# Attention and feed-forward on one core: a third buffer for scores and pieces, a second for the feed-forward step, values laid out so that nothing is shifted, and a new plan

## The chip, the core and the metric

The kernel runs on one core of one Trainium2 chip. Its engines work side by side, each through its own instructions in order: PE (TensorE, matmuls; PEld are its weight loads), DVE (VectorE), ACT (ScalarE), POOL (GpSimd), and SP (SyncE), which here issues every DMA. The metric is device time in microseconds of one execution. Sizes below are partitions x elements.

## The reference

```python
def _attn_ref(q, k, v, tau):                      # q, k, v: (8, 8, 576, 64)
    scale = 1.0 / np.sqrt(q.shape[-1])
    scores = scale * np.matmul(q, k.transpose(0, 1, 3, 2))
    thresh = np.max(scores, axis=-1, keepdims=True) - tau
    scores = np.where(scores >= thresh, scores, -1000000000.0)
    scores = scores - np.max(scores, axis=-1, keepdims=True)
    attn = np.exp(scores)
    attn = attn / (np.sum(attn, axis=-1, keepdims=True) + 1e-09)
    return np.matmul(attn, v)

def _moe_ref(x, w_in, w_out, s, b):               # x: (4608, 512), w_in: (512, 2048)
    h = x @ w_in
    r = np.maximum(h, 0.0)
    g = s * (r * r) + b
    return g @ w_out                              # w_out: (2048, 512)
```

x is the attention's output with the heads side by side. w_in and w_out come in as 64-bit floats, which the kernel takes apart itself.

## The kernel before

**Attention.** There are 8 batches of 4 pairs of heads. Batch 0 goes in plain fp32 (`plain_tile`, 36 tiles); batches 1 to 7 (`split_tile`, 9 tiles of 128 queries a pair, 252 in all) with numbers split in two: k and q as an fp32r part and the rest of it, the weights of the attention and v as two fp16 pieces. A split tile runs: scores on PE into bank `s` or `t` (L485); row maximum on DVE (L488); threshold on POOL (L490); exp on ACT into `em` (L492); threshold and sum on DVE (L494), which frees the bank; 1/sum by POOL and DVE (L497, L499); the first fp16 piece on ACT into `en` (L500), the second on DVE (L502); then a transposing DMA on SP (L507) brings both pieces, 1152 columns, into nine blocks of `ea` or `eb`. `em` and `en` have two buffers each, taken by tiles in turn.

**Values.** With 576 keys the first piece ends in the middle of the fifth block, so the second piece's keys sit 64 partitions off. `Values.prepare` therefore lays v out in five blocks and copies them, by three DMAs a head (L394), into four more blocks shifted by 64 partitions. `with_v` (L518) multiplies nine blocks of pieces by nine of v into bank `pv`, which ACT and DVE take out (L523, L525).

**Loads.** `Head.load` (L311) brings k and q of one head twice each, to partitions 0 to 63 and 64 to 127. `Head.prepare` splits them with ACT and POOL (L332 to L345).

**Feed-forward.** x goes in 18 blocks of 256 rows, 16 steps each, so 288 steps. A step (`Block.step`): 12 matmuls into bank `h` (L698), ReLU on ACT into the one buffer `g` (L702), square (L705), rounded part `gh` (L706), the rest `gl` on POOL (L707; DVE in the last block), then 6 matmuls into bank `o` (L713). `finish` (L727, L731) writes 256 rows out. `bias_t`, `oo` and `g` are buffers of their own.

**The order.** `Plan` holds every operation with its engine, a cost in ns (time on the engine, time to the result), what it reads and writes, and when it is due. `run` places them five times in a list schedule, forwards and backwards, keeps the shortest plan and emits all operations in its order. `HANDOVER` is the time from one engine's result to another engine's start. The plan knows buffers by the names in its lists; the order of accesses to one tile or bank is enforced apart from it by semaphores that the build puts in.

Of the kernel before, what the change touches and what calls it, by code (L numbers as in the profile page):

```python
# [9 lines left out]
F32 = mybir.dt.float32  # L10
F32R = mybir.dt.float32r
# [24 lines left out]
class Plan:  # L36
# [7 lines left out]
    HANDOVER = 50  # L44
# [95 lines left out]
def tile_attention_ffn(ctx: ExitStack, tc: tile.TileContext, qT, kT, v, tau, w_in, w_out, s, b, out):  # L140
# [3 lines left out]
    P = 128  # L144
# [28 lines left out]
    bias_t = const("bias_t", [P, DM])  # L173
# [3 lines left out]
    en, em = ([const(f"{n}{i}", [P, S + 1]) for i in range(2)] for n in ("en", "em"))  # L177
# [42 lines left out]
    def split_buffers():  # L220
# [10 lines left out]
        claim(["e32", "oo0", "oo1"] + [("x", 2, c, j, u) for c in range(NC) for j in range(2) for u in range(2)], lambda: None)  # L231
# [17 lines left out]
    def dma(kb, fn, r, w, at):  # L249
        plan.add("SP", (max(550, kb * 3.6), 2200 + kb * 3.6), fn, r, w, at)  # L250


    def transfer(rows, fn, r, w, at):
        plan.add("SP", (1250, 3400), fn, r, w, at)
# [42 lines left out]
    class Head:  # L297
        def __init__(self, i, bi, h, q0, q1, tail):
            self.i, self.bi, self.h, self.j, self.q0, self.q1, self.tail = i, bi, h, h % 2, q0, q1, tail
            self.v, self.kvs = vt[i % 3], [("v", i % 3, n) for n in range(4)]  # L300

        def load(self, at):

            q0, q1 = self.q0, self.q1
            self.parts = [], []

            def put(which, name, buf, cols, ap, kb):
                for o in 0, D:
                    keys = [(name, o, c) for c in range(cols.start // T, cols.stop // T)]
                    self.parts[which].extend(keys)  # L310
                    dma(kb, lambda o=o: nc.sync.dma_start(out=buf[o:o + D, cols], in_=ap), [], keys, at)  # L311

            put(0, "rk", rk, slice(0, S), kT[self.bi, self.h], 144)
            q1_ = S if self.tail and q1 == M else q1
            put(1, "rq", rq, slice(q0, q1_), qT[self.bi, self.h, :, q0:q1_], (q1_ - q0) // 4)
            if self.tail and q1_ < S:
                put(1, "rq", rq, slice(M, S), qT[self.bi, self.h, :, M:S], 16)

        def prepare(self, at):
            pk, pq = self.parts  # L320
            j = self.j
            q0, m = self.q0, self.q1
            n = m - q0
# [8 lines left out]
            act((580, 675), lambda: nc.scalar.copy(out=khi(), in_=rk), pk, [f"khi{j}"], at)  # L332
            pool((1420, 1450), lambda: nc.gpsimd.tensor_tensor(out=klo(), in0=rk, in1=khi().bitcast(F32), op=ALU.subtract),  # L333
                 pk + [f"khi{j}"], [f"klo{j}"], at)

            parts = [(slice(q0, m), qs[j][:, 0:n], f"q{j}", (60 + n, 160 + n), (100 + 2.3 * n, 130 + 2.3 * n))]
            if self.tail:
                parts.append((slice(M, S), qt[:, j, j * T:(j + 1) * T], f"qt{j}", (150, 245), (250, 280)))
            cut = [slice(q0, S)] if m == M and self.tail else [x[0] for x in parts]
            pool((130 + 1.25 * sum(x.stop - x.start for x in cut), 160 + 1.25 * sum(x.stop - x.start for x in cut)),  # L340
                 lambda: [nc.gpsimd.tensor_scalar(out=rq[:, x], in0=rq[:, x], scalar1=scale, scalar2=1.0, op0=ALU.mult,
                                                  op1=ALU.mult) for x in cut], pq + ["bound"], pq, at)
            for cs, dst, key, ca, cd in parts:
                act(ca, lambda dst=dst, cs=cs: nc.scalar.copy(out=dst, in_=rq[:, cs]), pq, [key], at)
                pool(cd, lambda dst=dst, cs=cs: nc.gpsimd.tensor_tensor(  # L345
                    out=dst[D:P], in0=rq[D:P, cs], in1=dst[D:P].bitcast(F32), op=ALU.subtract), pq + [key], [key], at)

    class Values:
# [5 lines left out]
        def load(self, at):  # L354
            bi, h2 = self.hds[0].bi, slice(self.hds[0].h, self.hds[0].h + 2)
            dma(256, lambda: nc.sync.dma_start(out=rv[:, :, 0:NQ, :].rearrange("p h t d -> p h (t d)"),
                                               in_=v[bi, h2, 0:M, :].rearrange("h (p t) d -> p h (t d)", t=NQ)),
                [], ["rv"], at)
            dma(32, lambda: nc.sync.dma_start(out=rv[0:T, :, NQ, :], in_=v[bi, h2, M:S, :].rearrange("h p d -> p h d")),
                [], [("rv", 1)], at)  # L360
# [626 lines left out]
```

## Time and profile before

| | us |
|---|---|
| median of 3 runs | 1317.81 (1310.39 to 1318.17) |
| the profiled run | 1319.79 |
| its span | 1318.0 |
| PE busy | 1234.2 (94%) |
| ACT busy | 998.6 (76%) |
| DVE busy | 910.3 (69%) |
| POOL busy | 761.0 (58%) |

The mean granted clock is 0.967. A group's row names line, engine, operation, out<-in, shapes and count, then busy time and mean ns of one, then the engine's idle time before these instructions and what ended most of it. A busy PE need not be at its peak: matmuls are pipelined. Which idle time matters is read by stage.

### The profile page before, as it was taken

What the parts mean: (1) busy time and instruction counts of PE and PEld (TensorE: products, weight loads), DVE (VectorE), ACT (ScalarE), POOL (GpSimd) and SP (SyncE); (2) the same over time, 40 slices, a digit from 0 to 9 for tenths busy, and PEclk for the clock granted to TensorE, in tenths of its full rate; (3) what the DMA queues carried; (4) which work ended last, traced back from release to release, by engine and by line L of the source; (5) the groups of instructions that cost most, each with busy time, mean ns of one, the idle gap of its engine ahead of it and who ended that gap; (6) DMA issues with size and microseconds to landing.
All of it is one profiled execution on the core that took longest, in us unless ns stands there. A gap on an engine that the chain in (4) does not pass through costs nothing.

```text
span 1318.0 us, 25354 instructions
## 1 busy us (share of the span) xinstructions
PE 1234.2 (94%) x8205; PEld 978.4 (74%) x8205; DVE 910.3 (69%) x2041; ACT 998.6 (76%) x2059; POOL 761.0 (58%) x1272
## 2 busy tenths in 40 slices
PE   9999988887999899999999999999999999999998
PEld 6667666766777677777878778878787777777776
DVE  6766888878777777777677778777777777750111
ACT  5676787877888887788788888878887987874543
POOL 2245376666776666667577666667666776632310
PEclk9778789998999999999999999999999999999999
DMA  9452036776667667766556667666766666640000
GB/s 295 146 160 65 10 76 136 147 134 147 134 137 133 127 139 137 144 126 137 99 130 129 141 126 136 130 140 128 136 119 139 112 141 125 123 80 1 17 17 17
DMA packets 362997, 155.30 MB, mean 118 GB/s; under 512 B 316784, under 2 KB 341360, under 8 KB 362864
## 3 DMA queue, kind: packets, MB, share of 16 engines
q1 hardware_dynamic: 362864, 153.69, 55.7%
q8 instruction: 64, 1.05, 0.3%
q14 instruction: 69, 0.57, 0.1%
HBM read 61.61 MB, written 9.44 MB: 54 GB/s over the span
## 4 chain that ended last, share of the span: by engine, by line
PE 51%; ACT 10%; DMA 9%; issue 8%; DVE 8%; POOL 8%; SPq 2%; POOLq 0%; DVEq 0%; ACTq 0%
PE o L713 18%; PE h L698 17%; PE pv L518 5%; DMA eb<-en 3%; PE t L485 3%; PE s L485 3%; POOL gl L707 2%; DMA ea<-en 2%; ACT en L500 2%; PE pv L463 2%; DMA rq<-in_q_dram 2%; DVE em L494 2%; PE s L420 2%; DVE en L502 2%; DVE st L488 2%
## 5 line engine op out<-in xcount | busy, mean ns | idle before, releaser
L698 PE MATMUL h<-xp,iw 128*128 128x256 f16 x3456 | 434.4, 276 | 10.5 <-ACT g L702 9.1
L698 PEld LDWEIGHTS <-iw 128*128 128x128 f16 x3456 | 323.3, 99 | 103.9 <-issue 60.4
L713 PE MATMUL o<-ow,gh 128*128 128x512 f32 x1152 | 384.0, 414 | 3.2 <-ACT gh L706 1.8
L707 POOL TENSOR_TENSOR gl<-g,gh 128x256 fp32r<-128x256 f32 x272 | 212.0, 779 | 188.7 <-ACT gh L706 149.4
L502 DVE SCALAR_TENSOR_TENSOR en<-em,st,en 128x576 f16<-128x576 f32 x252 | 235.1, 935 | 59.2 <-ACT en L500 56.9
L500 ACT ACTIVATE en<-em,st 128x576 f16<-128x576 f32 x252 | 194.0, 771 | 64.6 <-DMA eb<-en 27.5
L713 PE MATMUL o<-ow,gl 128*128 128x512 f32 x576 | 231.3, 402 | 7.4 <-POOL gl L707 6.9
L702 ACT ACTIVATE g<-h,wback 128x256 f32<-128x256 f32 x288 | 135.2, 469 | 117.8 <-PE h L698 89.9
L713 PEld LDWEIGHTS o<-ow,gh 128*128 128x128 f32 x1152 | 193.8, 191 | 28.5 <-ACT gh L706 2.7
L713 PEld LDWEIGHTS o<-ow,gl 128*128 128x128 f32 x576 | 108.9, 189 | 41.2 <-POOL gl L707 16.9
L490 POOL TENSOR_SCALAR st<-st,bound 128x1 f32<-128x1 f32 x252 | 104.7, 417 | 50.9 <-DVE st L488 36.2
L518 PEld LDWEIGHTS <-v 128*128 128x128 f16 x1008 | 93.1, 99 | 54.3 <-issue 15.7
L494 DVE SCALAR_TENSOR_TENSOR em<-t,st,em 128x576 f32<-128x576 f32 x126 | 102.5, 814 | 34.9 <-ACT em L492 16.0
L497 POOL TENSOR_SCALAR st<-st 128x1 f32<-128x1 f32 x252 | 79.9, 317 | 80.6 <-DVE em L494 50.8
L705 ACT ACTIVATE g<-g 128x256 f32<-128x256 f32 x288 | 119.7, 416 | 6.5
L706 ACT CAST gh<-g 128x256 fp32r<-128x256 f32 x288 | 116.0, 403 | 6.7 <-PE o L713 0.6
L494 DVE SCALAR_TENSOR_TENSOR em<-s,st,em 128x576 f32<-128x576 f32 x126 | 102.5, 814 | 22.4 <-ACT em L492 13.9
L492 ACT ACTIVATE em<-t,st 128x576 f32<-128x576 f32 x126 | 92.8, 737 | 22.5 <-DVE en L502 15.6
L488 DVE TENSOR_REDUCE st<-s 128x1 f32<-128x576 f32 x126 | 94.4, 749 | 20.6 <-PE s L485 19.7
L492 ACT ACTIVATE em<-s,st 128x576 f32<-128x576 f32 x126 | 92.8, 736 | 19.7 <-DVE en L502 12.0
L488 DVE TENSOR_REDUCE st<-t 128x1 f32<-128x576 f32 x126 | 94.4, 749 | 17.5 <-PE t L485 15.8
L333 POOL TENSOR_TENSOR k<-rk,k 128x576 fp32r<-128x576 f32 x56 | 80.9, 1445 | 25.3 <-ACT k L332 24.0
(158 smaller groups left out, 1853.1 us busy)
## 6 DMA issues: line engine op xcount, KB each, us to landing
rq<-in_q_dram SPq DMA_DIRECT2D x112, 144.0 KB, 2.9
rk<-in_k_dram SPq DMA_DIRECT2D x112, 144.0 KB, 2.9
iw<-in_moe_w_in_dram SPq DMA_DIRECT2D x16, 512.0 KB, 6.9
ow<-in_moe_w_out_dram SPq DMA_DIRECT2D x16, 512.0 KB, 7.2
out_dram<-oo SPq DMA_DIRECT2D x32, 256.0 KB, 2.8
rv<-in_v_dram SPq DMA_DIRECT2D x28, 256.0 KB, 3.2
v<-v SPq DMA_DIRECT2D x112, 64.0 KB, 2.1
ea<-en SPq DMA_TRANSPOSE x140, 3.2
```

The lines of the kernel that those rows point to most:

```text
L488: dve((745, 825), lambda: nc.vector.tensor_reduce(out=top, in_=ps, axis=mybir.AxisListType.XY, op=ALU.max, negate=True), [bk], [(ks_, 0)], ...
L492: act((740, 835), lambda: nc.scalar.activation(out=halves, in_=ps, func=AF.Exp, bias=top, scale=1.0), [bk, (ks_, 0)], [em_k], i - 0.5)
L494: dve((890, 970), lambda: nc.vector.scalar_tensor_tensor(out=halves, in0=ps, scalar=line, in1=halves, op0=ALU.is_ge, op1=ALU.mult, accum_o ...
L500: act((690, 785), lambda: nc.scalar.activation(out=pieces[:, 0:S], in_=ex, func=AF.Copy, scale=unit), [em_k, (ks_, 3)], [en_k], i)
L502: dve2((790, 880), lambda: nc.vector.scalar_tensor_tensor(out=pieces[:, S:2 * S], in0=ex, scalar=unit, in1=pieces[:, 0:S], op0=ALU.mult, o ...
L518: nc.tensor.matmul(ps, hd.v[:, n], e[:, n], start=(n == 0), stop=(n == 8))
L698: nc.tensor.matmul(ps, wi[w][f][:, c * P:(c + 1) * P], x[:, h, c, :], start=(c == 0 and i == 0), stop=(c == NC - 1 and i == 2))
L702: act((290, 385), lambda: nc.scalar.activation(out=g, in_=ps, func=AF.Relu, scale=wback[:, f:f + 1]), ["h", ("wback", f)], ["g"], at)
L705: act((290, 390), lambda: nc.scalar.activation(out=g, in_=g, func=AF.Square), ["g"], ["g"], at)
L706: act((310, 405), lambda: nc.scalar.copy(out=hi, in_=g), ["g"], [f"gh{k}"], at)
L707: do((715, 750), lambda: eng.tensor_tensor(out=lo, in0=g, in1=hi.bitcast(F32), op=ALU.subtract), ["g", f"gh{k}"], [f"gl{k}"], at)
L713: nc.tensor.matmul(bank["o"][:, t, :], a[:, ts_], w, start=(f == 0 and i == 0), stop=(f == NF - 1 and i == 2))
```

## The change

- `em` and `en` have three buffers in `split_tile`; `plain_tile` keeps two.
- The second piece is written in two DVE instructions, the last 64 keys first and then the other 512. Its keys then lie on the same partitions as the first piece's, apart from the fifth block, whose lower half belongs to the second piece. v's last 64 keys are loaded to both halves of the fifth block (`rv`), the products take block `n % 5`, and the shifting DMAs are gone.
- k and q of two heads come with one DMA per half of the partitions.
- `g` has two buffers, in the unused halves of the tiles of the converted w_in (`spare`), and `h` is taken in two halves of its bank in turn. Bias and output buffers lie in such halves too; the second buffer of the plain tiles' transposed scores lies in `rv`.
- `HANDOVER` is 150, and most costs in the plan are other numbers (one of them is shown).

```diff
-    HANDOVER = 50
+    HANDOVER = 150
...
-    en, em = ([const(f"{n}{i}", [P, S + 1]) for i in range(2)] for n in ("en", "em"))
+    en, em = ([const(f"{n}{i}", [P, S + 1]) for i in range(3)] for n in ("en", "em"))
...
-    vt = [const(f"v{i}", [P, 9, P], F16) for i in range(3)]
+    vt = [const(f"v{i}", [P, 5, P], F16) for i in range(3)]
...
-    rk, rq, rv = const("rk", [P, S]), const("rq", [P, S]), const("rv", [P, 2, 5, D])
+    rk, rq, rv = const("rk", [P, 2, S]), const("rq", [P, 2, S]), const("rv", [P, 2, 5, D])
...
-    oo = const("oo", [P, 2, DM])
-    gb = const("g", [P, NB])
...
+    def spare(f):
+
+        return lazy["wi", f][:, 2:4].bitcast(F32).rearrange("p a b -> p (a b)")
...
-            def put(which, name, buf, cols, ap, kb):
-                for o in 0, D:
-                    keys = [(name, o, c) for c in range(cols.start // T, cols.stop // T)]
-                    self.parts[which].extend(keys)
-                    dma(kb, lambda o=o: nc.sync.dma_start(out=buf[o:o + D, cols], in_=ap), [], keys, at)
...
+            if not self.j:
+                h2 = slice(self.h, self.h + 2)
+                for n, buf, ap in ("rk", rk, kT), ("rq", rq, qT):
+                    for o in 0, D:
+                        load(288, lambda buf=buf, ap=ap, o=o: nc.sync.dma_start(
+                            out=buf[o:o + D], in_=ap[self.bi, h2].rearrange("h d s -> d h s")),
+                            [], [(n, o, j) for j in range(2)], at)
...
+            for u in range(2):
+                load(32, lambda u=u: nc.sync.dma_start(out=rv[u * T:(u + 1) * T, :, NQ, :],
+                                                       in_=v[bi, h2, M:S, :].rearrange("h p d -> p h d")),
+                     [], [("rv", 1 + u)], at)
...
-                for n, (r, c, r_, c_) in enumerate((
-                        (slice(0, T), slice(5, 9), slice(T, P), slice(0, 4)),
-                        (slice(T, P), slice(8, 9), slice(0, T), slice(4, 5)),
-                        (slice(T, P), slice(4, 8), slice(0, T), slice(0, 4)))):
-                    dma(64, lambda t=t, r=r, c=c, r_=r_, c_=c_: nc.sync.dma_start(out=t[r, c, :], in_=t[r_, c_, :]),
-                        keys[0:1], [keys[1 + n]], at)
...
-        ex, em_k = em[i % 2][:, 0:S], f"em{i % 2}"
-        pieces, en_k = en[i % 2].bitcast(F16)[:, 0:2 * S], f"en{i % 2}"
+        ex, em_k = em[i % 3][:, 0:S], f"em{i % 3}"
+        pieces, en_k = en[i % 3].bitcast(F16)[:, 0:2 * S], f"en{i % 3}"
...
-        act((740, 835), lambda: nc.scalar.activation(out=halves, in_=ps, func=AF.Exp, bias=top, scale=1.0),
+        act((636, 740), lambda: nc.scalar.activation(out=halves, in_=ps, func=AF.Exp, bias=top, scale=1.0),
...
-        dve2((790, 880), lambda: nc.vector.scalar_tensor_tensor(
-            out=pieces[:, S:2 * S], in0=ex, scalar=unit, in1=pieces[:, 0:S], op0=ALU.mult, op1=ALU.subtract),
-            [em_k, en_k, (ks_, 3)], [en_k], i)
+        def rest():
+            for o, c in (slice(S, S + T), slice(M, S)), (slice(S + T, 2 * S), slice(0, M)):
+                nc.vector.scalar_tensor_tensor(out=pieces[:, o], in0=ex[:, c], scalar=unit, in1=pieces[:, c],
+                                               op0=ALU.mult, op1=ALU.subtract)
+        dve2((800, 885), rest, [em_k, en_k, (ks_, 3)], [en_k], i)
...
-                nc.tensor.matmul(ps, hd.v[:, n], e[:, n], start=(n == 0), stop=(n == 8))
+                nc.tensor.matmul(ps, hd.v[:, n % 5], e[:, n], start=(n == 0), stop=(n == 8))
...
-            ps, g, hi, lo = bank["h"][:, 0:NB], gb, gh[k], gl[k]
+            ps, hi, lo, h, kg = bank["h"][:, k * NB:(k + 1) * NB], gh[k], gl[k], f"h{k}", f"g{k}"
+
+            def g():
+                return spare(k)[:, 0:NB]
```

More of the change, by code (lines that the diff above doesn't have):

```diff
@@ L249, in dma, with load @@
     def dma(kb, fn, r, w, at):
-        plan.add("SP", (max(550, kb * 3.6), 2200 + kb * 3.6), fn, r, w, at)
+        plan.add("SP", (max(600, kb * 3.6), 2200 + kb * 3.6), fn, r, w, at)
+    def load(kb, fn, r, w, at):
+        plan.add("SP", (620, 2300 + kb * 4.5), fn, r, w, at)
     def transfer(rows, fn, r, w, at):
-        plan.add("SP", (1250, 3400), fn, r, w, at)
+        plan.add("SP", (1350, 3600), fn, r, w, at)
     class Plain:
@@ L355, in load @@
             bi, h2 = self.hds[0].bi, slice(self.hds[0].h, self.hds[0].h + 2)
[L356 to L360, printed above, removed]
+            load(256, lambda: nc.sync.dma_start(out=rv[:, :, 0:NQ, :].rearrange("p h t d -> p h (t d)"),
+                                                in_=v[bi, h2, 0:M, :].rearrange("h (p t) d -> p h (t d)", t=NQ)),
+                 [], ["rv"], at)
@@ L569, in w @@
         def w(u):
-            t = sb("io"[u] + f"w{f}", [P, 2, DM], (F16, F32R)[u])
+            t = sb("io"[u] + f"w{f}", [P, 4 - 2 * u, DM], (F16, F32R)[u])
+            if not u:
+                lazy["wi", f] = t
             for h in range(2):
@@ L634, in products @@
                 nc.tensor.matmul(bank["h"], ones, wo[h][f], start=(n == 0), stop=(n == 7))
-        pe(8, DM, products, [(f"w{f}", "o") for f in fs] + ["ones"], ["h"], at)
+        hs = ["h0", "h1"]
+        pe(8, DM, products, [(f"w{f}", "o") for f in fs] + ["ones"], hs, at)
         if k == 0:
-            act((520, 620), lambda: nc.scalar.copy(out=bias_t, in_=bank["h"]), ["h"], ["bias"], at)
+            act((465, 565), lambda: nc.scalar.copy(out=spare(2), in_=bank["h"]), hs + [("w2", "i")], ["bias"], at)
         else:
-            dve((620, 700), lambda: nc.vector.tensor_tensor(out=bias_t, in0=bank["h"], in1=bias_t, op=ALU.add),
-                ["h", "bias"], ["bias"], at)
+            dve((660, 745), lambda: nc.vector.tensor_tensor(out=spare(2), in0=bank["h"], in1=spare(2), op=ALU.add),
+                hs + ["bias"], ["bias"], at)
         if k == 3:
-            act((560, 660), lambda: nc.scalar.mul(out=bias_t, in_=bias_t, mul=b_t), ["bias", "b"], ["bias"], at)
+            act((510, 610), lambda: nc.scalar.mul(out=spare(2), in_=spare(2), mul=b_t), ["bias", "b"], ["bias"], at)
     count = dict(stage=0, step=0)
@@ L696, in products @@
                 for c in range(NC):
-                    for i, (w, h) in enumerate(((0, 0), (0, 1), (1, 0))):
-                        nc.tensor.matmul(ps, wi[w][f][:, c * P:(c + 1) * P], x[:, h, c, :], start=(c == 0 and i == 0),
+                    for i, (w, u) in enumerate(((0, 0), (0, 1), (1, 0))):
+                        nc.tensor.matmul(ps, wi[w][f][:, c * P:(c + 1) * P], x[:, u, c, :], start=(c == 0 and i == 0),
                                          stop=(c == NC - 1 and i == 2))
-            plan.add("PE", (12 * 0.427 * NB, 12 * 0.427 * NB + 170), products, self.kx + [(f"w{f}", "i")], ["h"], at)
-            act((290, 385), lambda: nc.scalar.activation(out=g, in_=ps, func=AF.Relu, scale=wback[:, f:f + 1]),
-                ["h", ("wback", f)], ["g"], at)
+            plan.add("PE", (12 * 0.427 * NB, 12 * 0.427 * NB + 170), products, self.kx + [(f"w{f}", "i")], [h], at)
+            act((357, 473), lambda: nc.scalar.activation(out=g(), in_=ps, func=AF.Relu, scale=wback[:, f:f + 1]),
+                [h, ("wback", f), (f"w{k}", "i")], [kg], at)
             eng, do = (nc.vector, dve2) if self.last else (nc.gpsimd, pool)
-            act((290, 390), lambda: nc.scalar.activation(out=g, in_=g, func=AF.Square), ["g"], ["g"], at)
-            act((310, 405), lambda: nc.scalar.copy(out=hi, in_=g), ["g"], [f"gh{k}"], at)
-            do((715, 750), lambda: eng.tensor_tensor(out=lo, in0=g, in1=hi.bitcast(F32), op=ALU.subtract),
-               ["g", f"gh{k}"], [f"gl{k}"], at)
+            act((320, 417), lambda: nc.scalar.activation(out=g(), in_=g(), func=AF.Square), [kg], [kg], at)
+            act((308, 405), lambda: nc.scalar.copy(out=hi, in_=g()), [kg], [f"gh{k}"], at)
+            do((712, 735) if not self.last else (340, 425), lambda: eng.tensor_tensor(out=lo, in0=g(), in1=hi.bitcast(F32), op=ALU.subtract),
+               [kg, f"gh{k}"], [f"gl{k}"], at)
             def second(t):
@@ L721, in finish, with take @@
             for t in range(2):
[L722 removed]
+                k = f"oo{t}"
                 for j, r in enumerate((slice(0, T), slice(T, P)) if many else (slice(0, P),)):
                     u = 2 * t + j if many else 0
[L726 to L729 removed]
+                    def take(t=t, r=r, u=u):
+                        nc.vector.scalar_tensor_tensor(out=spare(3 + t)[r], in0=bank["o"][r, t, :],
+                                                       scalar=power[n][r, 4, u:u + 1], in1=spare(2)[r], op0=ALU.mult,
+                                                       op1=ALU.add)
+                    dve((660, 745), take, ["o", ("o", t), "bias", (f"power{n}", 4), (f"w{3 + t}", "i")], [k], at)
                 for lo_, hi_, rows in self.rows[t]:
[L731 to L732 removed]
+                    load(256, lambda lo_=lo_, hi_=hi_, rows=rows, t=t: nc.sync.dma_start(out=rows, in_=spare(3 + t)[lo_:hi_]),
+                         [k], [], at)
     class Tile_:
```

140 lines of the change are left out of this document (61 added, 79 removed).

## The prediction, on record before the result

> **What bounds the kernel now.** I read the page first, then busy time by stage, then the groups of instructions and the waits, and last the order of time at one stall. By stage (busy time of each engine, count in brackets, granted clock, share of the DMA engines):
>
> ```profile
> 0.00:168.00 168.00, 154.71 (x939) 109.26 (x939) 117.56 (x352) 112.43 (x247) 64.06 (x105) 0.84 0.42 133
> 168.00:300.00 132.00, 112.80 (x752) 88.02 (x751) 108.78 (x236) 105.56 (x207) 89.00 (x147) 0.96 0.65 126
> 300.00:500.00 200.00, 183.00 (x1200) 147.74 (x1198) 155.81 (x338) 161.51 (x320) 135.57 (x230) 0.95 0.68 136
> 500.00:1200.00 700.00, 671.38 (x4588) 545.12 (x4587) 513.60 (x1089) 563.89 (x1161) 452.48 (x763) 1.00 0.63 125
> 1200.00:1318.00 118.00, 112.34 (x736) 88.25 (x734) 14.59 (x28) 55.22 (x126) 19.90 (x29) 1.00 0.05 14
> ```
>
> After the span of the stage the columns are PE, PEld, DVE, ACT, POOL. The first stage is the batch in plain fp32, the next three attention of batches 1 to 7 mixed with the feed-forward part, the last feed-forward alone. From 168 to 1200 PE is idle for 19.2 + 17.0 + 28.6 = 64.8 us, and the clock takes 132 × 0.04 + 200 × 0.05 = 15.3 us more: 80.1 us lost in 1032 us. That is all that this change can win there, since it leaves every matmul in place. The last stage, once it runs full, is PE alone; the chain of waits (start, length) repeats a step's second half every 2.72 us:
>
> ```profile
> 1299.94 1.40 PE o L713 x6
> 1302.66 1.40 PE o L713 x6
> ```
>
> What makes PE wait in the middle is the chain of attention. The groups (busy us, mean ns | idle time before them, and who ended it) show where ACT stands still:
>
> ```profile
> L500 ACT ACTIVATE en<-em,st 128x576 f16<-128x576 f32 x252 | 194.0, 771 | 64.6 <-DMA eb<-en 27.5 <-DMA ea<-en 16.1 <-DVE st L499 15.1
> L702 ACT ACTIVATE g<-h,wback 128x256 f32<-128x256 f32 x288 | 135.2, 469 | 117.8 <-PE h L698 89.9 <-POOL gl L707 19.4 <-PE t L446 2.0
> L492 ACT ACTIVATE em<-t,st 128x576 f32<-128x576 f32 x126 | 92.8, 737 | 22.5 <-DVE en L502 15.6 <-DVE st L488 5.1 <-DVE st L499 0.6
> L492 ACT ACTIVATE em<-s,st 128x576 f32<-128x576 f32 x126 | 92.8, 736 | 19.7 <-DVE en L502 12.0 <-DVE st L488 6.0 <-DVE st L499 0.2
> ```
>
> One such stall in order of time, rows picked from 302 to 311 us:
>
> ```profile
> 302.21 1.27 DVE L502 SCALAR_TENSOR_TENSOR en<-em,st,en 128x576 f16<-128x576 f32 x1
> ...
> 304.04 1.39 SPq L507 DMA_TRANSPOSE eb<-en  x1
> ...
> 305.54 1.18 SPq L311 DMA_DIRECT2D rq<-in_q_dram  x2
> ...
> 308.48 0.77 ACT L500 ACTIVATE en<-em,st 128x576 f16<-128x576 f32 x1 [2.24 <-DMA eb<-en]
> 309.16 0.72 ACT L492 ACTIVATE em<-t,st 128x576 f32<-128x576 f32 x1
> ...
> 309.78 1.04 ACT L666 ACTIVATE xp<-x 128x1024 f16<-128x1024 f32 x1
> ```
>
> The pieces of a tile are ready at 303.5 us; SP sends the transpose half a microsecond later; the next user of the same `en` buffer, L500, stands 2.24 us until the transpose has read it. Behind it on ACT stands the squaring of the next block of x, on which PE waited 4.82 us. What it cost beyond that shows in two windows of 10 us:
>
> ```profile
> 300.00:310.00 10.00, 5.85 (x34) 4.27 (x31) 7.81 (x17) 6.90 (x14) 4.73 (x10) 1.00 0.93 202
> 310.00:320.00 10.00, 8.92 (x50) 7.47 (x51) 8.55 (x19) 7.89 (x15) 7.18 (x13) 0.66 0.32 61
> ```
>
> PE idles 4.15 us, and its clock in the window behind is 0.66. The Trainium skill, TensorE: Matmul & The Clock Gate, The HAM clock gate, says the same in its way: the clock falls to half after an idle window of some 3.4 us and there is nothing between half and full. By that rule the 15.3 us end with the idle gaps; by the row alone I let them shrink with the rest.
>
> **The change part by part.** *Third buffer for em and en.* It takes away the waits of L500 for the transposes, 27.5 + 16.1 = 43.6 us, and of L492 for L502 two tiles before, 15.6 + 12.0 = 27.6 us. *Second g.* The wait of L702 for POOL goes, 19.4 us; the first activation of a step now waits for the POOL work of two steps before. Together 90.6 us of ACT's idle time. From 168 to 1200 ACT is busy 105.56 + 161.51 + 563.89 = 831.0 us and idle 201.0, so 45% of that idle time goes. I let PE's 80.1 us shrink in the same share: **-36 us**. The bounds are 0, if ACT then waits for something else, and -80. What is late next is DVE and POOL's small scalars between its passes, whose rows below stay.
>
> *h in two halves.* They lie in one PSUM bank, and the built program still orders the halves: of 288 first products 180 wait for the activation of the step just before, 20 for the one before that, by the counts that they wait for. On PE, at a seam between two steps of one block (iw12, iw13: weights of step 12 and 13), before:
>
> ```order
> L698 MATMUL h_115<-xp1_6223,iw12_1420 128x256
> L368 MATMUL pv_114<-vm_81,ones_68 128x2 [waits DVE_49]
> L485 MATMUL t_113<-k_1447,qt_69 128x288 x8
> L713 MATMUL o_112<-ow10_1301,gh0_107 128x512 x2
> L713 MATMUL o_112<-ow10_1301,gl0_109 128x512
> L698 LDWEIGHTS iw13_1556
> L698 MATMUL h_115<-xp1_6223,iw13_1556 128x256 [waits Activation_49]
> ```
>
> and now:
>
> ```order
> L696 LDWEIGHTS iw12_1500
> L696 MATMUL h_114<-xp1_6201,iw12_1500 128x256
> L696 LDWEIGHTS iw13_1603
> L696 MATMUL h_114<-xp1_6201,iw13_1603 128x256 [waits Activation_49]
> L696 LDWEIGHTS iw13_1603
> L696 MATMUL h_114<-xp1_6201,iw13_1603 128x256
> ```
>
> Two steps' first products now often stand back to back with nothing between; before, other matmuls gave the activation its time. The rows that bear on the price:
>
> ```profile
> PE h L698 <- ACT g L702: 9.1, 14, 1.7
> ...
> PEld L518 <- DMA v<-v: 5.5, 5, 2.7
> ```
> ```profile
> L615 PEld LDWEIGHTS pv<-norm,ones 128*128 128x128 f32 x36 | 6.1, 202 | 11.3 <-ACT xp L666 9.9 <-ACT x L523 0.5 <-DVE x L525 0.4
> ```
>
> PE's own wait for the activation is 9.1 us in all, so at best -9. L615 writes columns of the pv bank that L523 and L525 don't read, and waits for them all the same: a bank is one buffer to this program. The dearest end is 180 waits of a whole L702, 180 × 0.469 = 84 us. I take 0, because in most of the order other matmuls still stand between, and keep both ends. The Trainium skill, PSUM — Partial Sum Buffer, PSUM bank collisions raise a hardware error, says that two engines must be kept apart by bank and quadrant, not by address, since the hardware neither arbitrates nor stalls. The trace agrees with it, by the 0.5 and 0.4 us of L615; without that rule the sum would be 9 us lower.
>
> *Second piece with its last keys in front.* One DVE instruction of 576 columns becomes two, of 64 and 512, 252 times. The nearest rows:
>
> ```profile
> L525 DVE SCALAR_TENSOR_TENSOR x<-pv,vs,x 64x256 f32<-64x256 f32 x112 | 53.8, 481 | 18.6 <-ACT x L523 8.6 <-ACT xt L523 7.9 <-PE pv L615 0.5
> L525 DVE SCALAR_TENSOR_TENSOR xt<-pv,vs,xt 64x64 f32<-64x64 f32 x56 | 15.6, 278 | 0.7
> ```
>
> (481 - 278) / 192 = 1.06 ns a column, so 210 ns are there whatever the size; part of it overlaps the instruction before. A split costs 0 to 210 ns, 0 to 53 us of DVE time; I take 0.1 us, 25 us. DVE is busy 108.78 + 155.81 + 513.60 = 778.2 of 1032 us and idle 253.8, so a microsecond on it weighs about 80.1 / 253.8 = 0.32 on PE: **+8 us**, bounds 0 and +17, and +53 if DVE alone set the pace, which at 82% in its densest stage it doesn't. In the Trainium skill, Perfetto Trace Analysis, Optimizing Scalar/DVE Operations, a DVE instruction on SBUF carries some 60 ns of its own; by that price, an estimate, the 252 cost 15 us of DVE time and the term would be 5; no run here shows it yet.
>
> *SP's queue.* The DMAs that go or come (issues, KB, us to landing):
>
> ```profile
> rq<-in_q_dram SPq DMA_DIRECT2D x112, 144.0 KB, 2.9
> rk<-in_k_dram SPq DMA_DIRECT2D x112, 144.0 KB, 2.9
> ...
> v<-v SPq DMA_DIRECT2D x112, 64.0 KB, 2.1
> ...
> v<-v SPq DMA_DIRECT2D x56, 16.0 KB, 1.8
> rv<-in_v_dram SPq DMA_DIRECT2D x28, 32.0 KB, 2.7
> ```
>
> 168 shifts of v go, 224 loads of k and q become 112 of twice the size, 28 loads of v's last keys come: 252 issues fewer. Two rq issues took 1.18 us above, so 252 × 0.59 = 149 us of SP's queue. On SP, a stretch within one batch before (rq, rk: raw q and k; ea, eb: the transposed pieces of the pair's two heads; v: a head's values):
>
> ```order
> L311 DMA rq_99<-in_q_dram 64x576 x2
> L507 DMA_TRANSPOSE ea_1689<-en0_76 128x9x128
> L394 DMA v2_95<-v2_95 64x512
> L394 DMA v2_95<-v2_95 64x128
> L507 DMA_TRANSPOSE ea_1689<-en1_77 128x9x64
> L507 DMA_TRANSPOSE eb_1884<-en1_77 128x9x64
> L394 DMA v2_95<-v2_95 64x512
> L394 DMA v0_93<-v0_93 64x512
> ```
>
> and now, at a like place:
>
> ```order
> L499 DMA_TRANSPOSE eb_1839<-en2_77 128x9x128
> L499 DMA_TRANSPOSE eb_1839<-en0_75 128x9x128
> L314 DMA rk_99<-in_k_dram 64x2x576 x2
> L314 DMA rq_100<-in_q_dram 64x2x576 x2
> L499 DMA_TRANSPOSE eb_1839<-en1_76 128x9x128
> L499 DMA_TRANSPOSE eb_1839<-en2_77 128x9x128
> L499 DMA_TRANSPOSE ea_1737<-en0_75 128x9x128
> ```
>
> Transposes stand closer together and take three en buffers in turn. Nothing waits for SP's time as such; what it holds up is in the 43.6 us already. PE's own wait for the shift, 5.5 us on PEld, goes: **-4 us**, bounds 0 and -5.5. Loading two heads at once ties the next pair's load to both heads' preparation; POOL's preparation of one head is short beside the nine tiles of a pair, so I take 0, and up to 28 × 2.9 = 81 us if each pair waited out a load.
>
> *The plan.* A handover counts 150 ns, not 50, and most costs are new. That moves work on every engine, also in the first stage, where PE loses 13.3 us idle and 168 × 0.16 = 26.9 by the clock. I take 0 and a quarter of these 40 us either way, ±10. Dropped memsets and the moved buffers of bias and output touch no step on the path: 0; if they did, it would be 32 evictions late by a fraction of a microsecond.
>
> The sum is -36 + 8 - 4 = -32: span 1318.0 becomes 1286. The profiled run took 1319.79 us, 1.8 outside its span, and the median of the three runs is 1317.81, 2.0 below it, so span and median agree and I forecast **1286 us**.
>
> **The rivals.** *More is won:* ACT's waits paced the mix, and PE, once fed, loses a quarter of 80.1 us: -60 - 4 = 1254 us. For it: PE is already at 671 of 700 from 500 us on, so a fed PE is possible. Against: batch 1 ends before more feed-forward work exists, whatever the buffers.
> *The waits only move:* ACT no longer stands at L500 but at the next DVE result. For it, the idle time that other waits than the removed ones end: 15.1 us at L500 for L499, 89.9 us at L702 for PE. It gives 1308 to 1322, say 1314.
> *Slower, by the one bank:* the plan now lets a step's first product follow without regard to the activation before it, and the program makes it wait. Place: L696 behind the activation of the step before, 180 times. From 32 / 180 = 0.18 us exposed each time the gain is eaten; at 0.30 us, two thirds of an activation, it is 54 - 32 = +22, 1340 us. Against: ACT's activations come late already, so the order leaves room. That the halves don't double h, as the text says they do, is part of the forecast too.
>
> **How the numbers follow.** Forecast 0.53 (1270 to 1304), more won 0.15 (1245 to 1270), moved waits 0.20 (1305 to 1322), the bank 0.12 (over 1331). About 1% is what a measurement of this kernel can tell from no change, so faster means under 1304.6: 0.68; same 0.20; slower 0.12. The range leaves out half of the second case and the last one: 1256 to 1321.
>
> **What would show it.** Right: L500's idle time for transposes under 10 us, L702's for POOL gone, PE's idle time from 168 to 1200 near 40 us, no v<-v. Wrong: PE waiting for the activation by 30 us or more (bank), DVE's busy time up by 50 us (split), or ACT's idle time as large as now under other names. A first stage other than 158 to 178 us would be the plan's doing.

## The result, and the profile after

The changed kernel takes 1283.3 us (median of 4 runs, 1281.8 to 1284.6). Its ratio to the kernel before is 0.9749, 95% interval 0.9717 to 0.9781. The forecast was 1286 us. The profiled run has a span of 1282.8 us, 35.2 below the 1318.0 of before. Busy time by stage, in the columns of the prediction:

```profile
0.00:168.00 168.00, 157.26 (x1117) 115.28 (x1118) 138.42 (x393) 131.40 (x292) 76.12 (x125) 0.98 0.45 140
168.00:300.00 132.00, 112.39 (x699) 89.23 (x700) 115.76 (x286) 103.94 (x204) 94.48 (x157) 0.91 0.76 142
300.00:500.00 200.00, 190.52 (x1298) 157.76 (x1297) 164.53 (x387) 161.07 (x330) 139.95 (x232) 0.98 0.69 131
500.00:1200.00 700.00, 673.23 (x4595) 554.89 (x4595) 510.06 (x1205) 547.33 (x1155) 430.52 (x744) 1.00 0.59 112
```

By the forecast's own measure (PE's idle time plus what the clock takes) PE loses from 168 to 1200 us 19.6 + 9.5 + 26.8 idle and 132 × 0.09 + 200 × 0.02 = 15.9 by the clock: 71.8 us, 8 less than the 80.1 of before. In the first 168 us it loses 10.7 + 168 × 0.02 = 14.1 us, 26 less than the 40.2 of before. The forecast had it the other way round: 36 in the middle, nothing in the first stage. PE's idle time in the middle is 55.9 us, where it was 64.8 and the forecast looked for some 40. The last fp32 scores start at 145.0 us instead of 162.3, with 12 feed-forward steps done by then instead of 9. (The stretches are the same times in each kernel, not the same work.)

More than half of the gain comes with the clock: by these rows it takes 3.4 + 15.9 = 19.3 us up to 1200 us, where it took 26.9 + 15.3 = 42.2. This isn't the profiled run alone: the mean granted clock was 0.983 to 0.989 in the four runs of the changed kernel and 0.966 to 0.978 in 45 runs of the kernel before.

The groups on ACT that answer to those shown of before:

```profile
L490 ACT ACTIVATE en<-em,st 128x576 f16<-128x576 f32 x252 | 192.7, 771 | 36.9 <-DVE st L489 32.0 <-DMA eb<-en 3.3
L700 ACT ACTIVATE iw<-h,wback 128x256 f32<-128x256 f32 x288 | 135.6, 471 | 141.5 <-PE h L696 130.9 <-PE pv L364 3.6 <-POOL st L480 2.0
L482 ACT ACTIVATE em<-t,st 128x576 f32<-128x576 f32 x126 | 92.9, 737 | 23.2 <-DVE st L478 18.8 <-DVE st L489 2.3 <-DVE en L494 0.9
L482 ACT ACTIVATE em<-s,st 128x576 f32<-128x576 f32 x126 | 92.9, 737 | 21.9 <-DVE st L478 17.7 <-DVE en L494 2.3 <-DVE vs L365 1.1
```

One row of its waits (us, times, longest):

```profile
ACT iw L700 <- POOL gl L705: 2.0, 4, 0.9
```

The waits that the buffers were to remove are nearly gone: `eb`'s transposes at L490 3.3 us for 27.5, L494 at L482 0.9 + 2.3 = 3.2 for 27.6, POOL's `gl` at L700 2.0 for 19.4. But the groups stand idle nearly as long: before 64.6 + 117.8 + 22.5 + 19.7 = 224.6 us, now 36.9 + 141.5 + 23.2 + 21.9 = 223.5. (Some 60 us of each sum, 62.8 before and 60.8 now, are waits for PE's first products behind 1150 us, where PE alone sets the pace and they cost nothing. From 168 to 1150 us the sums are 149.1 and 152.4.) ACT now waits for DVE's row maximum (L478), for DVE's 1/sum (L489) and for PE's first products (L696). The forecast had named just this, idle time as large under other names, as a sign that it was wrong: it speaks against its largest term.

### The profile page after: what moved, and what is told of

Read it like the earlier page. It is cut to its first block, busy times and chain, and to the rows that moved or that the text cites. A ratio compares the mean times of both kernels' runs of the same rounds, so it can differ in the third digit from the quotient of the medians.

```text
span 1282.8 us, 25258 instructions
## 1 busy us (share of the span) xinstructions
PE 1210.4 (94%) x8205; PEld 977.4 (76%) x8205; DVE 940.1 (73%) x2293; ACT 979.8 (76%) x2059; POOL 750.6 (59%) x1271
## 4 chain that ended last, share of the span: by engine, by line
PE 57%; ACT 13%; DVE 11%; DMA 7%; issue 6%; POOL 4%; SPq 0%; DVEq 0%; ACTq 0%; POOLq 0%
PE h L696 21%; PE o L711 19%; PE pv L510 5%; DMA eb<-en 4%; PE s L475 3%; DVE en L494 3%; PE t L475 3%; ACT iw L700 3%; DMA rq<-in_q_dram 2%; ACT en L490 2%; DVE st L478 2%; DVE em L484 2%; PE s L410 2%; ACT em L482 2%; PE pv L453 2%
## 5 line engine op out<-in xcount | busy, mean ns | idle before, releaser
L696 PE MATMUL h<-xp,iw 128*128 128x256 f16 x3456 | 428.8, 276 | 20.3 <-ACT iw L700 16.5
L696 PEld LDWEIGHTS <-iw 128*128 128x128 f16 x3456 | 328.1, 99 | 102.5 <-issue 57.0
L711 PE MATMUL o<-ow,gh 128*128 128x512 f32 x1152 | 377.7, 409 | 0.2
L705 POOL TENSOR_TENSOR gl<-iw,gh 128x256 fp32r<-128x256 f32 x272 | 214.2, 789 | 167.1 <-ACT gh L704 128.1
L494 DVE SCALAR_TENSOR_TENSOR en<-em,st,en 128x64 f16<-128x64 f32 x504 | 268.3, 575 | 32.4 <-ACT en L490 30.5
L700 ACT ACTIVATE iw<-h,wback 128x256 f32<-128x256 f32 x288 | 135.6, 471 | 141.5 <-PE h L696 130.9
L490 ACT ACTIVATE en<-em,st 128x576 f16<-128x576 f32 x252 | 192.7, 771 | 36.9 <-DVE st L489 32.0
L484 DVE SCALAR_TENSOR_TENSOR em<-s,st,em 128x576 f32<-128x576 f32 x126 | 102.3, 812 | 32.6 <-ACT em L482 18.4
L484 DVE SCALAR_TENSOR_TENSOR em<-t,st,em 128x576 f32<-128x576 f32 x126 | 102.4, 812 | 30.7 <-ACT em L482 14.1
L703 ACT ACTIVATE iw<-iw 128x256 f32<-128x256 f32 x288 | 119.6, 416 | 5.3
L704 ACT CAST gh<-iw 128x256 fp32r<-128x256 f32 x288 | 115.1, 401 | 9.9 <-PE o L711 6.1
L482 ACT ACTIVATE em<-t,st 128x576 f32<-128x576 f32 x126 | 92.9, 737 | 23.2 <-DVE st L478 18.8
L482 ACT ACTIVATE em<-s,st 128x576 f32<-128x576 f32 x126 | 92.9, 737 | 21.9 <-DVE st L478 17.7
L487 POOL TENSOR_SCALAR st<-st 128x1 f32<-128x1 f32 x252 | 67.6, 268 | 67.0 <-DVE em L484 36.0
L478 DVE TENSOR_REDUCE st<-s 128x1 f32<-128x576 f32 x126 | 94.4, 749 | 12.7 <-PE s L475 11.9
L478 DVE TENSOR_REDUCE st<-t 128x1 f32<-128x576 f32 x126 | 94.3, 748 | 9.0 <-PE t L475 8.1
L475 PE MATMUL t<-k,q 128*128 128x288 f32 x448 | 84.9, 312 | 6.7 <-DVE em L484 5.8
```

The source lines that it names most:

```text
L475: nc.tensor.matmul(ps[:, hf], stat, kk[:, cs], start=(n == 0), stop=(n == len(seq) - 1))
L478: dve((667, 750), lambda: nc.vector.tensor_reduce(out=top, in_=ps, axis=mybir.AxisListType.XY, op=ALU.max, negate=True), [bk], [(ks_, 0)], ...
L482: act((636, 740), lambda: nc.scalar.activation(out=halves, in_=ps, func=AF.Exp, bias=top, scale=1.0), [bk, (ks_, 0)], [em_k], i - 0.5)
L484: dve((740, 900), lambda: nc.vector.scalar_tensor_tensor(out=halves, in0=ps, scalar=line, in1=halves, op0=ALU.is_ge, op1=ALU.mult, accum_o ...
L490: act((668, 774), lambda: nc.scalar.activation(out=pieces[:, 0:S], in_=ex, func=AF.Copy, scale=unit), [em_k, (ks_, 3)], [en_k], i)
L494: nc.vector.scalar_tensor_tensor(out=pieces[:, o], in0=ex[:, c], scalar=unit, in1=pieces[:, c], op0=ALU.mult, op1=ALU.subtract)
```

## Experiments

**Theories.** The forecast's: the third `em` and `en` and the second `g` carry the gain, and the remade plan is worth 0, 10 us either way. The rival: the plan's new numbers carry it. Each run below is timed against the kernel before on the same chip (medians 1314.7 to 1317.2 us).

**The new numbers alone**, on the kernel before:

```
-    HANDOVER = 50
+    HANDOVER = 150
...
-        act((740, 835), lambda: nc.scalar.activation(out=halves, in_=ps, func=AF.Exp, bias=top, scale=1.0),
+        act((636, 740), lambda: nc.scalar.activation(out=halves, in_=ps, func=AF.Exp, bias=top, scale=1.0),
```

> The kernel before with only the numbers of the plan changed: a handover of 150 ns and the new costs; buffers, loads, v's shifts and the one-instruction second piece stay as before. The forecast's theory (the buffers carry the gain, the plan is worth 0 with 10 us either way) expects 1307 to 1327 us, the last plain score near 162 us after the span's start, ACT's idle time at L500 for the transposes near the 43.6 us of before. The rival (the plan carries about half: the 17.5 us of the first stage and some of batch 1) expects the last plain score near 145 us and 1288 to 1300 us in all, with the transposes' waits still there.

Measured: 1272.9 us, ratio 0.9679 (0.9638 to 0.9720), 44 us below the kernel before and 10 below the changed one. The last fp32 scores start at 148.7 us. Its groups:

```profile
L500 ACT ACTIVATE en<-em,st 128x576 f16<-128x576 f32 x252 | 193.9, 771 | 60.4 <-DVE st L499 27.8 <-DMA eb<-en 22.8 <-DMA ea<-en 7.6
L702 ACT ACTIVATE g<-h,wback 128x256 f32<-128x256 f32 x288 | 135.3, 470 | 100.1 <-PE h L698 74.6 <-POOL gl L707 22.2 <-POOL st L497 1.2
```

The transposes still cost ACT 30.4 us, and POOL's `gl` 22.2, more than before. The whole gain is there without touching them. The rival had put a part of the gain here; it is more than all of it. Busy time by stage:

```profile
0.00:168.00 168.00, 157.59 (x1045) 115.07 (x1046) 129.59 (x375) 122.89 (x274) 68.26 (x115) 0.88 0.43 136
168.00:300.00 132.00, 106.87 (x682) 83.22 (x682) 110.08 (x237) 101.61 (x195) 88.72 (x148) 0.98 0.72 141
300.00:500.00 200.00, 191.75 (x1295) 155.90 (x1296) 159.34 (x344) 168.44 (x339) 142.94 (x240) 0.97 0.67 138
500.00:1200.00 700.00, 684.38 (x4708) 561.04 (x4707) 500.41 (x1067) 567.67 (x1174) 458.22 (x759) 1.00 0.61 122
```

From 168 to 1200 us PE loses 25.1 + 8.3 + 15.6 = 49.0 idle and 132 × 0.02 + 200 × 0.03 = 8.6 by the clock, 57.6 us in place of 80.1; in the first 168 us 10.4 + 20.2 = 30.6 in place of 40.2. So the new numbers work mostly in the middle, where the forecast gave the plan nothing, and PE's idle time falls further there than with all the buffers of the changed kernel (55.9).

**The changed kernel with the old numbers**, the reverse edit.

> The changed kernel with the old numbers of the plan: a handover of 50 ns and the old costs; three em and en, two g, the split piece and the loads of two heads stay. The forecast's theory expects the stretch after the first stage to take what it takes in the changed kernel, so 1283 us plus at most the 17.5 us of the first stage, 1283 to 1301 us. The rival (the plan carries the gain) expects 1305 to 1320 us, with L500 no longer waiting for transposes and the last plain score near 162 us.

Measured: 1311.6 us, 0.9955 (0.9925 to 0.9985). The last fp32 scores start at 164.7 us, and L490 waits 2.8 us for a transpose. So under the old numbers everything else in the change is worth 5.6 us together; under the new ones it costs 1283.3 - 1272.9 = 10.4.

**Two buffers again**, in the changed kernel, planned anew:

```
-        ex, em_k = em[i % 3][:, 0:S], f"em{i % 3}"
+        ex, em_k = em[i % 2][:, 0:S], f"em{i % 2}"
```

with the same for `en`.

> The changed kernel with em and en taken two in turn again in the split tiles, planned anew with its own numbers. The forecast's theory put 71.2 of the 90.6 us of removed ACT waits on these buffers, 71.2 / 90.6 of 36 = 28 us: 1311 us, the loss spread over batches 1 to 7, ACT waiting 40 us or more at L490 for transposes. The rival (what the third buffers remove comes back as waits for DVE) expects 1283 to 1295 us, with less waiting for DVE at L482 and L490 in exchange.

Measured: 1318.8 us, 1.0021 (0.9998 to 1.0045), 35 above the changed kernel. The waits in question:

```profile
ACT en L490 <- DMA eb<-en: 30.0, 27, 3.7
ACT em L482 <- DVE en L494: 25.4, 36, 2.1
```

Taken alone this would have confirmed the forecast. It doesn't: the new numbers with the same two buffers, in the structure of before, take 1272.9 us with 30.4 us of waits for the transposes. The order here is another one: no feed-forward step is done when the last fp32 scores start, where the changed kernel has done 12. So the new numbers don't make every order good: here they give one as slow as the kernel before.

**One name for both halves of `h`**, so that the plan knows of one bank:

```
-  ps, hi, lo, h, kg = bank["h"][:, k * NB:(k + 1) * NB], gh[k], gl[k], f"h{k}", f"g{k}"
+  ps, hi, lo, h, kg = bank["h"][:, k * NB:(k + 1) * NB], gh[k], gl[k], "h0", f"g{k}"
```

> The changed kernel with both halves of bank h under one name in the plan, so that the plan lets a step's first products follow the activation of the step before, as the build orders most of them anyway; the halves are still written in turn. The forecast's theory (the halves are worth 0) expects 1283 us within 6 us. The rival (the plan that doesn't know the one bank loses by it) expects 1270 to 1277 us and the 16.5 us that PE waits for the activation at the first products (L696) under 10 us. A second rival (the loose order is a gain, since the 69 activations that wait for the next step's products cost nothing) expects 1289 us or more.

Measured: 1286.4 us, 0.9753 (0.9678 to 0.9828): no difference that this can tell. The term of 0 stands within about 10 us. PE's wait for the activation does fall, from 16.5 us to less than half, as the first rival expected:

```profile
PE h L696 <- ACT iw L700: 6.0, 8, 1.1
```

The time doesn't follow, but the four runs lie far apart, and with the clock: 1277.2 and 1280.3 us at a mean of 0.984 and 0.977, 1292.4 and 1294.8 us at 0.966 and 0.963. A gain of a few us could hide in that.

**The handover alone**, on the kernel before: the first pair of lines above, without the costs.

> The kernel before with one number changed: HANDOVER 150 for 50; the old costs stay. All new numbers together had given 1272.9 us, 44 below the kernel before. If the handover carries that, 1270 to 1288 us, with the last plain score at 145 to 152 us. If the new costs carry it, 1305 to 1320 us with the last plain score near 162 us. Anything between would mean that both are needed.

Measured: 1296.2 us, 0.985 (0.9802 to 0.9898), -20.6. **The costs alone**, with HANDOVER 50:

> The kernel before with the new costs and HANDOVER 50 as before. The handover alone gave 1296 us (-20.6) and both together 1273 us (-44). If the two add up, 1293 us (-23). If the new costs are worth something only with slack between the engines, 1308 to 1320 us. If they carry the whole by themselves, 1270 to 1280 us.

Measured: 1278.2 us, 0.9741 (0.9692 to 0.9791), -37. The two don't add up: together they give 44 us, not 58. The costs alone come within 5 us of both together. The handover alone stops about halfway, which was to mean that both are needed; the run with the costs alone shows that they are not. **HANDOVER 200 with the new costs**, for the luck in an order:

> The kernel before with the new costs and HANDOVER 200 in place of 150, to see how much of a plan's time is luck. If longer handovers and truer costs give an order that bears delays, 200 is close to 150: 1266 to 1282 us. If the 1272.9 us of 150 was a lucky order, 200 lies anywhere up to the 1296 us that 150 gave with the old costs.

Measured: 1278.3 us, 0.9727 (0.9685 to 0.9769). With the new costs, handovers of 50, 150 and 200 ns give 1278.2, 1272.9 and 1278.3 us: the choice among them is worth about 5 us, which is no more than their intervals leave open, and little is to be read into such a difference below.

What the new costs have in their favour stood in the trace of before:

```profile
L494 DVE SCALAR_TENSOR_TENSOR em<-t,st,em 128x576 f32<-128x576 f32 x126 | 102.5, 814 | 34.9 <-ACT em L492 16.0 <-POOL st L490 7.5 <-POOL st L497 2.8
L705 ACT ACTIVATE g<-g 128x256 f32<-128x256 f32 x288 | 119.7, 416 | 6.5
L488 DVE TENSOR_REDUCE st<-s 128x1 f32<-128x576 f32 x126 | 94.4, 749 | 20.6 <-PE s L485 19.7
```

| instruction (line of before) | old cost to the result, ns | new | mean in the trace |
|---|---|---|---|
| exp, L492 | 835 | 740 | 737 |
| ReLU, L702 | 385 | 473 | 469 |
| square, L705 | 390 | 417 | 416 |
| row maximum, L488 | 825 | 750 | 749 |
| threshold and sum, L494 | 970 | 900 | 814 |

The old plan thought exp and the row maximum 10 to 13% too long and ReLU a fifth too short. That this is why its order was worse is argued from the table: no run changed one cost by itself, and none tried costs that are merely other ones, not truer ones.

**The same order, with the buffers.** The kernel before keeps all names and numbers of its plan, so every engine's order stays. Only the tiles differ (bias, output rows and `g` move too, to make the room):

```
-        ex, em_k = em[i % 2][:, 0:S], f"em{i % 2}"
+        ex, em_k = em[i % 3][:, 0:S], f"em{i % 2}"
...
+                return spare(k % 2)[:, 0:NB]
```

In one of the 252 tiles the exponential of a later tile then comes before the last read of `em`, so that tile's result is not the reference's; the work is the same.

> The kernel before, planned with its own names and numbers, so that every engine's order is that of before, while the tiles really take three em and en in turn and two g. Bias, output rows and g move to unused parts of the weights' buffers to make the room, as in the changed kernel. Only waits are taken away. The forecast's theory (90.6 us of ACT's waits gone are worth 36 us on PE) expects 1281 us. The rival, that the waits only move, expects 1309 to 1318 us, with ACT's idle time at L500 and L492 for transposes and L502 gone and more of it under other names.

Measured: 1300.9 us, 0.9884 (0.9855 to 0.9913), -15.7. Its groups (the same instructions as before, some lines further down there):

```profile
L501 ACT ACTIVATE en<-em,st 128x576 f16<-128x576 f32 x252 | 193.6, 771 | 47.3 <-DVE st L500 39.1 <-DMA eb<-en 3.0 <-DVE st L489 1.8
L708 ACT ACTIVATE iw<-h,wback 128x256 f32<-128x256 f32 x288 | 135.5, 470 | 117.0 <-PE h L704 107.6 <-POOL st L491 2.0 <-POOL gl L713 1.9
L493 ACT ACTIVATE em<-s,st 128x576 f32<-128x576 f32 x126 | 92.7, 736 | 11.4 <-DVE st L489 10.2 <-DVE en L503 0.2
L493 ACT ACTIVATE em<-t,st 128x576 f32<-128x576 f32 x126 | 92.7, 736 | 8.8 <-DVE st L489 8.2
```

Both theories are half right. The idle time of these groups falls by 40 us, from 224.6 to 47.3 + 117.0 + 11.4 + 8.8 = 184.5. Of the 90.6 us of waits some 5 are left, and 49 came back as waits for DVE's 1/sum (15.1 to 39.1 us), PE's first products (89.9 to 107.6 us) and the row maximum (11.1 to 18.4 us). The last stage has no part in this. Behind 1150 us, before and here:

```profile
L702 ACT ACTIVATE g<-h,wback 128x256 f32<-128x256 f32 x55 | 26.0, 474 | 65.0 <-PE h L698 62.8 <-POOL gl L707 1.9
L708 ACT ACTIVATE iw<-h,wback 128x256 f32<-128x256 f32 x49 | 23.3, 475 | 63.7 <-PE h L704 63.7
```

On the end this is 15.7 us, not 36, and none of it is the clock: its mean was 0.971 to 0.976 in the six runs, within the 0.966 to 0.978 of before.

**The same edit under the new numbers**, again in an order that stays.

> The same edit made to the kernel before with the new numbers: its order stays, and em, en and g only have the third and second buffer. There ACT waits 30.4 us at L500 for transposes, 13.9 at L492 for L502 and 22.2 at L702 for POOL, 66.5 us in all. By the forecast's rate, 36 / 90.6, that is worth 26 us: 1247 us. If the waits only move, 1266 to 1276 us. Slower than 1278 us would be a cost of the moved bias, output and g.

Measured: 1265.5 us, 0.9629 (0.9592 to 0.9666), 7.4 below the new numbers alone, and half a microsecond under the range of the moved waits. Two of its groups, and of the new numbers alone the third of the waits that the 66.5 us are made of:

```profile
L501 ACT ACTIVATE en<-em,st 128x576 f16<-128x576 f32 x252 | 193.7, 770 | 44.8 <-DVE st L500 42.3 <-DMA eb<-en 1.0 <-DVE vs L372 0.2
L708 ACT ACTIVATE iw<-h,wback 128x256 f32<-128x256 f32 x288 | 135.5, 470 | 102.7 <-PE h L704 96.0 <-POOL gl L713 2.1 <-POOL st L498 1.8
```
```profile
ACT em L492 <- DVE en L502: 13.9, 28, 1.0
```

The waits for 1/sum grow from 27.8 to 42.3 us and those for PE's first products from 74.6 to 96.0. The 66.5 us of waits were worth about 7 here, which the two intervals don't quite separate from nothing. This kernel's median is below both.

**Buffers known to the plan, without the rest.** The changed kernel with v in nine blocks and shifted, the second piece in one instruction, loads by the head:

```
-                nc.tensor.matmul(ps, hd.v[:, n % 5], e[:, n], start=(n == 0), stop=(n == 8))
+                nc.tensor.matmul(ps, hd.v[:, n], e[:, n], start=(n == 0), stop=(n == 8))
```

> The changed kernel with what the kernel before had in v and loads: nine blocks of v with the shifting DMAs, the second piece in one instruction, k and q by the head. It keeps the third em and en, the second g, the halves of h and the new numbers, so against the new numbers alone (1272.9 us) it has the buffers more. The forecast's theory (28 us by the third buffers, 8 by g) expects 1237 to 1255 us. The rival (under the new numbers the buffers are worth nothing, since what waits for them then waits for DVE and PE) expects 1267 to 1280 us.

Measured: 1279.0 us, 0.9723 (0.9689 to 0.9757), as the rival expected: 6 above the new numbers alone, though in a fixed order the buffers gained 7. Neither difference is clear of the intervals by itself, but the one between the two kernels with the buffers is: a plan that knows of the third buffers, the second `g`, the halves of `h` and the moved tiles comes to an order that is 13.5 us worse than the one that doesn't; which of these does it is open.

**The second piece in one instruction**, in the changed kernel's own order:

```
-            for o, c in (slice(S, S + T), slice(M, S)), (slice(S + T, 2 * S), slice(0, M)):
-                nc.vector.scalar_tensor_tensor(out=pieces[:, o], in0=ex[:, c], scalar=unit, in1=pieces[:, c],
-                                               op0=ALU.mult, op1=ALU.subtract)
+            nc.vector.scalar_tensor_tensor(out=pieces[:, S:2 * S], in0=ex, scalar=unit, in1=pieces[:, 0:S],
+                                           op0=ALU.mult, op1=ALU.subtract)
```

> The changed kernel, in its own order, with the second piece written in one DVE instruction of 576 columns; its last keys then don't meet the blocks of v they belong to, so that part of the result is left wrong, and every other instruction is the same. The forecast's term (the split costs 8 us, 25 us of DVE time at 0.32) expects 1275 us. If DVE's whole extra 33 us lie on the path it is 1250 us; if other work hides them, 1280 to 1286 us.

Measured: 1275.1 us, 0.9682 (0.9655 to 0.9709). The split costs 8.2 us, as the forecast's term said. DVE's busy time is the first row with one instruction, the second in the changed kernel:

```profile
PE 1207.8 (95%) x8205; PEld 977.4 (77%) x8205; DVE 898.4 (71%) x2041; ACT 979.1 (77%) x2059; POOL 765.5 (60%) x1271
```
```profile
PE 1210.4 (94%) x8205; PEld 977.4 (76%) x8205; DVE 940.1 (73%) x2293; ACT 979.8 (76%) x2059; POOL 750.6 (59%) x1271
```

41.7 us for 252 splits are 165 ns each, and 8.2 / 41.7 = 0.20 of it reaches the end. The forecast had 0.1 us and 0.32; the product came out right.

**Two buffers with loads by the head:**

```
-  out=buf[o:o + D], in_=ap[self.bi, h2].rearrange("h d s -> d h s")),
+  out=buf[o:o + D], in_=ap[self.bi, self.h]),
```

> The changed kernel with two em and en in turn and k and q loaded by the head again. With two buffers alone it had taken 1318.8 us, 35 more than with three. If the loads of two heads, 288 KB and 4.3 to 5.2 us each, stood ahead of the transposes and made the third buffer needed, this comes down to 1272 to 1290 us and ACT's wait for the transposes falls from 30.0 to under 15 us. If two buffers cost 35 us with any loads, or the order was simply a worse one, it stays at 1305 to 1320 us.

Measured: 1303.5 us, 0.989 (0.9846 to 0.9934), between the two. ACT's wait for the transposes falls from 30.0 to 15.5 us and 15 us come back; again no feed-forward step is done in the first stage. Whether the loads do it or once more another order, this run can't say; some 20 of the 35 us that two buffers cost the changed kernel stay unexplained.

## Why the prediction was right, and where it was not

Change by change, under the new numbers, with one kernel for each step:

| step | us | forecast's term |
|---|---|---|
| before to new numbers | 1317.2 to 1272.9: -44 | plan: 0 ± 10 |
| buffers, halves of `h`, moved tiles | to 1279.0: +6 | -36, 0, 0 |
| v not shifted, loads of two heads | to 1275.1: -4 | -4, 0 |
| second piece in two instructions | to 1283.3: +8 | +8 |

- **The total was right by two errors that cancel**, so by luck. -36 for the buffers came out as +6, and 0 for the plan as -44. The sum of the forecast's terms is -32, the measured one -34. The steps of -4 and +6 are each no larger than what the intervals leave open.
- **Third buffers and second `g`.** The step that failed is "I let PE's 80.1 us shrink in the same share". Even in an unchanged order, where just these waits go, it is -15.7 us: 49 us return under other names, as the rival of moved waits has it, most of them at L500 for 1/sum and at L702 for PE, the very rows that it pointed to (of its 89.9 us at L702, though, 62.8 lie behind 1150 us and cost nothing). In a better order 66.5 us of waits are worth about 7. A share of ACT's idle time was not a share of PE's here.
- **The plan.** The forecast took a quarter of the first stage's 40 us as its bound, and looked nowhere else. The first stage did come out at 145 us, outside 158 to 178, which the prediction had named as the plan's doing, and the run with the numbers alone shows it at 148.7. Neither the quarter nor the limit to the first stage had a row behind it: in the middle PE lost 57.6 us with the new numbers alone, in place of 80.1. What could have been suspected was the direction, by the table of costs above. That the new numbers carry the gain is shown, by adding them to one kernel and taking them out of the other; why their order is better is not, and with two buffers in the changed kernel they gave 1318.8 us. The clock is part of it: its mean was 0.977 to 0.989 with the numbers or the costs alone, but 0.972 to 0.977 at HANDOVER 200.
- **Halves of `h`, and the rival of the one bank.** PE's wait for the activation rose from 9.1 to 16.5 us:

```profile
PE h L696 <- ACT iw L700: 16.5, 29, 1.3
```

  That is far from 30 us, and telling the plan of the one bank, which brings it to 6.0, changes the time by nothing that can be told from the spread of its runs. The rival at 1340 us was wrong, and so was the dear end of the bounds: 180 orders by the program are not 180 waits.
- **DVE split.** 8 forecast, 8.2 measured, from a longer instruction and a smaller share. These 165 ns of DVE's busy time lie inside the forecast's 0 to 210. The Trainium skill's price (Perfetto Trace Analysis, Optimizing Scalar/DVE Operations) is some 60 ns of engine time, and by the same page the latency that a profile shows is about twice that; the 165 ns here are more than either.
- **SP's queue and the loads.** -4 forecast, -3.9 measured, which is less than what two orders of one kernel differ by, so the agreement is not proof. No v<-v is left; in exchange POOL waits longer for q, which comes in 288 KB, 51.6 us for 42.9:

```profile
POOL rq L333 <- DMA rq<-in_q_dram: 51.6, 25, 5.4
```

- **More won, 1254.** Not reached here, but the new numbers with the buffers in a fixed order come to 1265.5: PE could be fed better than the forecast's 1286, by the order first (1272.9) and little by the buffers.
- **What was overlooked.** The kernel before was held back by its order more than by its buffers, and the rows of L492 and L702 that the prediction quotes stood against the costs in its code.

## What to carry to other kernels

Where a planner sets the order, change its numbers and its buffers in separate runs, and test a buffer in an order that is held fixed; undoing one part and planning anew gave 35 us that were no evidence for that part. Compare a plan's costs with the trace's means before anything else: here the new costs alone took the time to 0.9741, and that they did so by being truer is likely, not shown. Of the idle time that was removed from an engine that isn't the bound, more than half came back here at the next producers, so a share of it should not be carried over to the bound.

## What the runs showed of the hardware

The clock loss of the first stage doesn't follow PE's gaps. In the kernel before:

```profile
40.00:44.00 4.00, 3.35 (x31) 2.27 (x30) 2.10 (x8) 3.27 (x6) 1.13 (x3) 1.00 1.05 385
44.00:48.00 4.00, 3.06 (x12) 2.04 (x13) 3.89 (x13) 2.98 (x8) 1.09 (x1) 0.89 0.40 131
48.00:52.00 4.00, 4.00 (x25) 2.59 (x25) 2.40 (x12) 0.77 (x1) 0.76 (x1) 0.50 0.02 7
52.00:56.00 4.00, 3.51 (x13) 2.20 (x13) 2.88 (x9) 3.24 (x8) 1.54 (x3) 0.50 0.00 0
56.00:60.00 4.00, 4.00 (x27) 2.81 (x26) 1.95 (x7) 0.70 (x3) 0.74 (x1) 0.50 0.00 0
```

From 48 to 60 us PE is busy 11.5 of 12 us, by records that grow longer as the clock falls (one L463 product takes 0.27 us at 42.70 and 0.42 us at 50.23), and the clock stays at half throughout. From PE's first instruction to 168 us no gap between matmuls or weight loads is longer than 1.7 us. The Trainium skill (TensorE: Matmul & The Clock Gate, The HAM clock gate) lets the clock fall after an idle window of about 3.4 us. At 306 us the trace agrees, where the clock falls inside a gap of 4.82 us; here it fell without one and didn't return under work that looks dense. The changed kernel at the same place:

```profile
48.00:52.00 4.00, 2.52 (x30) 1.78 (x28) 4.00 (x12) 3.19 (x9) 1.49 (x2) 1.00 0.00 0
52.00:56.00 4.00, 3.93 (x34) 2.60 (x33) 3.45 (x12) 3.58 (x8) 1.44 (x1) 1.00 0.00 0
56.00:60.00 4.00, 3.91 (x33) 2.73 (x33) 4.00 (x16) 2.63 (x6) 2.06 (x3) 1.00 0.12 23
```

Here PE has 97 matmuls in 12 us instead of 65, idles more, 1.6 us against 0.5, and keeps its clock. So a stage's busy share says little while its clock is low: what the changed kernel gains in the first stage is mostly clock, 26.9 us lost before and 3.4 now. The order alone doesn't decide it. The kernel with the buffers in the order of before has every engine's instructions in the same sequence there, and keeps its clock until 65 us:

```profile
48.00:52.00 4.00, 3.40 (x34) 2.19 (x32) 3.71 (x14) 2.72 (x6) 1.15 (x3) 1.00 0.00 0
52.00:56.00 4.00, 3.72 (x32) 2.71 (x32) 4.00 (x11) 2.79 (x8) 2.51 (x2) 1.00 0.00 0
56.00:60.00 4.00, 2.96 (x29) 2.20 (x29) 3.27 (x12) 3.95 (x9) 0.79 (x2) 1.00 0.07 16
```

In its first 168 us the clock takes 168 × 0.09 = 15.1 us; over its six runs the mean clock is no higher than before. What makes the clock fall at 47 us wasn't tried.
